# Batch 0's keys and queries by the software queue, cast on the way; memsets on VectorE; a written-out order table

## The chip, the cores and the metric

The kernel runs on one core of a Trainium2 chip. The metric is the device time of one execution in microseconds (us); three runs of the kernel before took 288.24 to 289.09 us, median 288.83 us. The core has five engines with an instruction stream each: PE (TensorE, matmuls), DVE (VectorE), ACT (ScalarE), POOL (GpSimd) and SP (SyncE). DMAs that SP issues go through a hardware queue (q1 in the profile), DMAs that POOL issues through a software queue (q0), whose descriptors POOL writes itself. Both queues share 16 DMA engines.

## The reference, cut to what matters

```python
def _attn_ref(q, k, v):                      # (8, 8, 576, 64): batch, heads, rows, head size
    scores = (1.0 / np.sqrt(D)) * np.matmul(q, k.transpose(0, 1, 3, 2))
    mask = block_i >= block_j                # blocks of 64 rows
    scores = np.where(mask, scores, -1e9)
    ...
    return np.matmul(softmax(scores), v)

def _moe_ref(x, w_tok1, w_tok2, w_ch1, w_ch2):   # x: (8, 576, 512), the heads side by side
    xt = x.transpose(0, 2, 1)
    h = np.maximum(xt @ w_tok1, 0.0) @ w_tok2    # over rows: 576 -> 256 -> 576
    u = x + h.transpose(0, 2, 1)
    h2 = np.maximum(u @ w_ch1, 0.0) @ w_ch2      # over channels: 512 -> 1536 -> 512
    return u + h2
```

All inputs and the output are float32 in DRAM. The kernel computes in bfloat16 with float32 sums.

## The kernel before

**The work.** Eight batches, each with attention over two groups of four heads (hg 0 and 1), a token mix and a channel stage of two products. For each head group, keys and queries lie as `qk_sb` tiles of 128 partitions (four heads, 32 partitions each) by 18 columns of 64 values, in bfloat16. DVE transposes them in blocks (`load_qk`, L540), by halves of nine columns. PE makes the scores in three sets (`score_set`, L664); ACT takes the exponential (`exp`, L682); PE multiplies with v (`head_out`, L712, and `ends_out`, L765); DVE divides by the row sum (L732, L738). Then come `token_up` (L906, L910), `first_uT` or `token_mix` (L939, L954, L1001), `channel_up` (L1125, later L1318) and the down products (L1547, L1452), whose results SP stores.

**Loads.** For batches 1 to 7, POOL issues one DMA per key or query tile (L517), and the DMA casts from float32 to bfloat16 on the way. For batch 0 (`first` in `load_qk`) SP issues nine float32 DMAs into staging tiles (L524; the stages are the `gT` tiles seen as float32, L350): halves of k and q, and the second half of q of hg 0 once more in two (edges 0, 9, 14, 18). ACT or DVE then casts each piece into `qk_sb` (L529, by way of the helper at L498 and L500), and DVE transposes it. All v (L566), token weights (L577) and channel weights (L600, L609) come by POOL's queue, cast on the way. At most eight POOL DMAs are in flight: the ninth waits for the landing of the first.

**Small things at the start.** POOL makes the identity (`make_identity`, L469), fills `bar` (two memsets), the pads of the first v tile (three) and the pads of the first token weight (two), all at L443, before it issues its first DMA. DVE fills `zeros` and the pads of the second v tile. `raise_clock` gives PE 16 matmuls over zeros (L469) and then up to 110 short ones of 256 columns (L476), "fillers", which stand in PE's stream where nothing else was ready.

**What sets the order.** `P.add` registers an op (a group of instructions on one engine) with its dependencies, a cost, a priority, and PSUM banks that it takes and gives. `Plan.placed` adds a table of shifts (`SHIFTS`) to the priorities and pins some ops to an engine (`ONLY`); `Plan.run` then goes through time by the costs, starts on each engine the ready op of best priority, and so fixes each engine's order, the engine of each op and its bank. The instructions are issued in that order, and each engine runs its own list in order; what the hardware waits for are semaphores. Fillers that found no room before 20 us are left out. The chip's real times do not change the order.

**Numbers of ops.** An op has the number of its `P.add` call. The text below uses the numbers of the table after the change, where the nine casts of batch 0 are gone and all later numbers are smaller by nine: 1, 3, 5, 7, 9 are the loads of hg 0 of batch 0 and 2, 4, 6, 8, 10 their transposes; 11, 13, 15, 17 the loads of hg 1 and 12, 14, 16, 18 their transposes; 19 to 23 and 24 to 28 the v loads; 29 to 39 the memsets, 40 the identity, 41 the 16 zero matmuls, 42 to 151 the fillers, 152 to 155 the token weights, 156 to 166 the channel weights, 171 and on the score sets, exponentials and head products of batch 0.

Of the kernel before, what the change touches and what calls it, by code (L numbers as in the profile page):

```python
# [11 lines left out]
FP32 = mybir.dt.float32  # L12
# [9 lines left out]
class Op:  # L22
# [3 lines left out]
        "engines", "cost", "deps", "emit", "prio", "take", "give", "xfer",  # L26
        "users", "need", "key", "waiting", "ready", "start", "end", "engine", "n", "mode", "at", "urgent", "until", "quick", "stick",
# [3 lines left out]
class Plan:  # L31


    LAG = {"PE": 0.28, "ACT": 0.2, "DVE": 0.18, "POOL": 0.22, "SP": 0.1}


    FIRST = {"POOL": 2.2, "ACT": 0.7, "SP": 0.7}
# [6 lines left out]
        for pool in pools  # L44
    }
# [8 lines left out]
    def add(  # L54
        self, engines, cost, emit, deps=(), prio=0.0, take=(), give=(), xfer=None, mode=0, at=0.0,
        urgent=0, until=1e9, quick=False, stick=False,
    ):

        o = Op()
        o.engines = (engines,) if isinstance(engines, str) else tuple(engines)  # L60
        o.cost = cost if isinstance(cost, dict) else {e: cost for e in o.engines}
        o.emit, o.prio, o.take, o.give, o.xfer = emit, prio, take, give, xfer
        o.mode, o.at, o.urgent, o.until, o.quick, o.stick = mode, at, urgent, until, quick, stick
        o.deps = list({id(d): d for d in deps if d is not None}.values())
        o.users, o.n = [], len(self.ops)
        self.ops.append(o)
        return o
# [4 lines left out]
    def fits(self, o, coming=()):  # L72
        for pools, n in o.need:
            have = sum(p in pools for p in coming)
            for p in pools:
                have += len(self.free[p])
            if have < n:
                return False
        return True

    def placed(self):

        letters = {"A": "ACT", "D": "DVE", "P": "POOL"}
        shifts, only = [int(x) for x in SHIFTS.split()], "".join(ONLY.split())
        assert len(self.ops) == len(shifts) == len(only)
        for o, shift, letter in zip(self.ops, shifts, only):
            o.prio += 0.05 * shift
            if letter in letters:
                o.engines = (letters[letter],)
        return self.run()  # L90

    def run(self):
        for o in self.ops:
            o.users = []
            o.need = [
                (pools, sum(set(other) <= set(pools) for other, _ in o.take)) for pools in {pools: 0 for pools, _ in o.take}
            ]
        for o in self.ops:
            o.waiting, o.ready = len(o.deps), o.at
            for d in o.deps:  # L100
                d.users.append(o)
        busy = {e: 0.0 for e in self.LAG}
        queued = [(o.at, o.n) for o in self.ops if not o.waiting]
        heapq.heapify(queued)

        avail = {e: [] for e in self.LAG}
        t, hard, soft, gives, order, mode = 0.0, 0.0, 0.0, [], [], 0
        left = len(self.ops)
        landed = [0.0] * 8

        fleeting = max([o.until for o in self.ops if o.until < 1e9], default=0.0)
        over = False
        while left:
            while queued and queued[0][0] <= t:
                o = self.ops[heapq.heappop(queued)[1]]
                o.key = (-o.urgent, o.prio, o.n, o)
                for e in o.engines:
                    bisect.insort(avail[e], o.key)
            while gives and gives[0][0] <= t:
                _, name, slot = heapq.heappop(gives)  # L120
                self.free[name].append(slot)
            began = False
            if not over:
                over = t > fleeting
                left -= sum(a[3].until < t for a in avail["PE"])
                avail["PE"] = [a for a in avail["PE"] if a[3].until >= t]
            for e in ("PE", "ACT", "DVE", "POOL", "SP"):
                if busy[e] > t or e == "POOL" and landed[-8] > t:
                    continue
                at = None  # L130
                tiled = e == "PE" and mode > 0
                for n, a in enumerate(avail[e]):
                    if a[3].stick > tiled or at is not None and not a[3].stick:
                        continue
                    if self.fits(a[3]):
                        at = n
                        if a[3].stick or not tiled:
                            break
                if at is None:
                    continue  # L140
                o = avail[e][at][3]
                soon = t + 0.6 * o.cost[e]
                if any(
                    r < soon and self.ops[n].urgent > o.urgent and e in self.ops[n].engines
                    for r, n in queued
                ):
                    continue
                if any(
                    -u[0] > o.urgent and self.fits(u[3], [name for r, name, _ in gives if r < soon])
                    for u in avail[e][:at]  # L150
                ):
                    continue
                for x in o.engines:
                    del avail[x][bisect.bisect_left(avail[x], o.key)]
                left -= 1
                began = True
                for pools, note in o.take:
                    note["pool"] = next(p for p in pools if self.free[p])
                    note["slot"] = self.free[note["pool"]].pop(0)
                o.engine, o.start = e, t  # L160
                o.end = busy[e] = t + o.cost[e] + 0.22 * sum(self.bare(note) for _, note in o.take)
                if o.mode is None:
                    o.mode = mode
                if e == "PE" and o.mode != mode:
                    o.end = busy[e] = o.end + 0.1
                    mode = o.mode
                order.append(o)
                lag = self.LAG[e]
                if o.xfer is not None:
                    first = o.end + self.FIRST[e]  # L170
                    if e == "POOL":
                        soft = max(soft, first) + o.xfer
                    else:
                        hard = max(hard, first) + o.xfer
                        soft += o.xfer * (soft > first)
                    o.end, lag = (soft if e == "POOL" else hard), 1.3
                    if e == "POOL":
                        landed.append(o.end + lag)
                for note in o.give:
                    to = self.TURN.get((note["pool"], note.get("covers")), note["pool"])  # L180
                    heapq.heappush(gives, (o.end + lag * (not o.quick), to, note["slot"]))
                for u in o.users:
                    same = u.engines == (e,) and o.xfer is None
                    u.ready = max(u.ready, o.end + ((e != "PE") * 0.05 if same else lag))
                    u.waiting -= 1
                    if not u.waiting:
                        heapq.heappush(queued, (u.ready, u.n))
            if not began:
                times = [b for b in busy.values() if b > t]
                times += [q[0] for q in queued[:1]] + [g[0] for g in gives[:1]] + landed[-8:]  # L190
                t = min(x for x in times if x > t)
        return order


SHIFTS = """
    0 0 0 1182 0 0 -172 0 0 186 0 0 -1226 0 0 1993 0 654 147 0 -1856 -1 0 -1627 2336 0 2272 -1123 -1113 -2707
    -2638 -1401 -798 -1583 -3531 -1120 -1939 -1736 0 0 0 0 0 -1021 -287 -489 0 0 0 0 0 0 0 0 0 0 0 0 0 0 0 0 0
    0 0 0 0 0 0 0 0 0 0 0 0 0 0 0 0 0 0 0 0 0 0 0 0 0 0 0 0 0 0 0 0 0 0 0 0 0 0 0 0 0 0 0 0 0 0 0 0 0 0 0 0 0
    0 0 0 0 0 0 0 0 0 0 0 0 0 0 0 0 0 0 0 0 0 0 0 0 0 0 0 0 0 0 0 0 0 0 0 0 0 0 0 0 0 0 0 0 0 -1629 -844 -738
    -987 -398 -755 -531 -696 -7 -19 -113 71 27 253 547 -2157 -341 -402 -3362 -1124 -1796 1135 -1317 2983 -860  # L200
    -4496 1412 484 -558 1057 -1890 -462 -3745 -4139 -1274 14 610 1601 3085 679 422 -1403 947 -248 2179 -1873
# [62 lines left out]
ONLY = """  # L264
# [17 lines left out]
def kernel(  # L282
# [11 lines left out]
    nc = tc.nc  # L294
# [1375 lines left out]
```

## Time and profile before

| what | value |
|---|---|
| time, three runs | 288.24, 288.83, 289.09 us |
| profiled execution: span from first to last instruction | 285.7 us (the page gives no other time of that execution; the median of the runs is 3.1 us above its span) |
| mean granted TensorE clock | 0.999 |
| PE busy | 280.5 us, 98% of the span |
| DVE, ACT, POOL busy | 234.5, 157.9, 69.6 us |
| software queue q0 | 44032 packets, 16.75 MB, 51.6% of 16 engines' span |
| hardware queue q1 | 20704 packets, 15.34 MB, 21.8% |

The page gives, for one execution, the busy time of each engine, the span in 40 slices, the DMA queues, and a chain of work followed back from the last instruction to whatever released each step. The trace can be asked for any stretch: a timeline lists instructions in order of time (start, duration, engine, line, operation, output<-input, and in brackets the idle time before it and what ended that), the chain of waits lists the steps of the chain (start, duration, what), and the view of a tile gives the time from the issue of its DMAs to their landing. A DMA instruction of POOL is busy while POOL writes descriptors; the data move later.

### The profile page before, as it was taken

The numbers are of one execution on the slowest core, as the hardware profiler recorded it, in microseconds if no ns is written. First come the engines' busy times: TensorE is split into PE (matmuls) and PEld (weight loads), VectorE is DVE, ScalarE is ACT, GpSimd is POOL, SyncE is SP. The second block draws the span as 40 slices with busy tenths as digits, with TensorE's granted clock in tenths as the row PEclk, the third lists the DMA queues.
The fourth block names the chain that finished last, engine by engine and source line by source line (L and its number), as shares of the span: only waits on it lengthen the run. The fifth ranks groups of instructions, "written<-read, shape, count | busy, mean of one in ns | idle before, by whom it ended". The sixth has DMA issues, their size and how long they took to land.

```text
span 285.7 us, 9042 instructions
## 1 busy us (share of the span) xinstructions
PE 280.5 (98%) x3923; PEld 188.2 (66%) x3923; DVE 234.5 (82%) x498; ACT 157.9 (55%) x212; POOL 69.6 (24%) x118
## 2 busy tenths in 40 slices
PE   8999999999999999999999999999999999999994
PEld 3676556565566856547876567744588985568883
DVE  3775788885699998479988588799996998999883
ACT  5986857568877458766475846335751037650000
POOL 8774545622251171701171001000000000000000
PEclk9999999999999999999999999999999999999999
DMA  8999999997499699942989006220080340000344
GB/s 228 215 165 208 213 182 186 206 183 151 66 100 105 82 197 204 187 54 22 136 137 199 6 2 76 76 92 2 19 129 2 117 179 0 0 2 0 149 127 169
DMA packets 64775, 32.65 MB, mean 114 GB/s; under 512 B 53088, under 2 KB 55264, under 8 KB 64736
## 3 DMA queue, kind: packets, MB, share of 16 engines
q0 software_dynamic: 44032, 16.75, 51.6%
q1 hardware_dynamic: 20704, 15.34, 21.8%
q8 instruction: 30, 0.49, 0.7%
q14 instruction: 9, 0.07, 0.1%
HBM read 35.85 MB, written 9.44 MB: 158 GB/s over the span
## 4 chain that ended last, share of the span: by engine, by line
PE 96%; DMA 1%; DVE 1%; SPq 0%; ACT 0%; issue 0%
PE mm L1452 17%; PE mm L1125 15%; PE sc L664 11%; PE late L1452 9%; PE mm L712 8%; PE late L1318 7%; PE mm L1318 6%; PE mm L906 5%; PE mm L1001 4%; PE mm L1547 4%; PE mm L765 2%; PE mm L1194 2%; DMA gT<-in_q_dram 1%; PE mm L910 1%; PE late L1194 1%; PE mm L476 1%
## 5 line engine op out<-in xcount | busy, mean ns | idle before, releaser
L682 ACT ACTIVATE e_sb<-sc 128x1024 bf16<-128x1024 f32 x95 | 92.4, 1023 | 40.9 <-PE sc L664 40.2
L540 DVE STREAM_TRANSPOSE qk_sb<-qk_sb 128x288 int32<-128x288 int32 (+1 forms) x65 | 41.2, 695 | 7.2 <-ACT qk_sb L498 4.0
L1125 PE MATMUL mm<-uT,wc_sb 128*128 128x512 bf16 x192 | 45.5, 381 | 0.0
L566 POOL DMA_DIRECT2D vals<-in_v_dram x45 | 37.2, 841 | 16.3 <-PE mm L712 7.3
L664 PE MATMUL sc<-qk_sb 32*64 32x64 bf16 (+7 forms) x1260 | 34.8, 293 | 0.2 <-DVE qk_sb L540 0.2
L1125 PEld LDWEIGHTS <-wc_sb 128*128 128x128 bf16 x192 | 20.2, 115 | 17.2 <-issue 1.3
L1452 PEld LDWEIGHTS <-sums 128*128 128x128 bf16 x288 | 27.7, 98 | 4.1 <-issue 0.9
L1452 PEld LDWEIGHTS <-gT 128*128 128x128 bf16 x288 | 27.5, 98 | 3.8
L664 PEld LDWEIGHTS <-qk_sb 32*64 32x64 bf16 x1280 | 19.6, 104 | 14.2 <-issue 9.0
L894 DVE TENSOR_SCALAR gT<-mm 128x512 bf16<-128x512 f32 x25 | 17.2, 687 | 13.9 <-PE mm L1125 13.2
L738 DVE TENSOR_TENSOR x_sb<-mm,rinv 128x256 bf16<-128x256 f32 x64 | 26.2, 421 | 1.5
L712 PE MATMUL mm<-vals,e_sb 128*128 128x65 bf16 x640 | 27.0, 193 | 0.1
L712 PEld LDWEIGHTS <-e_sb 128*128 128x128 bf16 x640 | 23.8, 97 | 4.8 <-issue 1.2
L892 ACT ACTIVATE gT<-mm 128x512 bf16<-128x512 f32 x35 | 20.5, 604 | 8.6 <-PE mm L1125 4.0
L498 ACT COPY mm<-late 128x512 f32<-128x512 f32 (+1 forms) x15 | 8.4, 563 | 26.3 <-PE late L1452 16.5
L906 PE MATMUL mm<-x_sb,w_sb 128*128 128x512 bf16 (+1 forms) x88 | 17.0, 321 | 0.0
L1016 DVE TENSOR_TENSOR u_sb<-mm,x_sb 128x512 bf16<-128x512 f32 x24 | 15.3, 680 | 1.4 <-PE mm L1001 1.2
L1452 PE MATMUL mm<-wd_sb,sums 128*128 128x256 bf16 x132 | 16.4, 273 | 0.0
L1318 PEld LDWEIGHTS <-ws_sb 128*128 128x128 bf16 x96 | 9.4, 98 | 9.9
L517 POOL DMA_DIRECT2D qk_sb<-in_k_dram x14 | 7.7, 553 | 32.8 <-DVE qk_sb L540 24.0
L1001 PE MATMUL mm<-aT,w_sb 128*128 128x512 bf16 x56 | 14.1, 380 | 0.0
L1452 PE MATMUL mm<-wc_sb,gT 128*128 128x256 bf16 x108 | 13.3, 273 | 0.0
(165 smaller groups left out, 481.8 us busy)
## 6 DMA issues: line engine op xcount, KB each, us to landing
out_dram<-o_sb SPq DMA_DIRECT2D x14, 512.0 KB, 3.4
qk_sb<-in_q_dram POOLq DMA_DIRECT2D x14, 288.0 KB, 6.3
qk_sb<-in_k_dram POOLq DMA_DIRECT2D x14, 288.0 KB, 6.9
vals<-in_v_dram POOLq DMA_DIRECT2D x28, 128.0 KB, 6.5
out_dram<-o_sb SPq DMA_DIRECT2D x7, 256.0 KB, 3.3
wc_sb<-in_moe_w_ch_dram POOLq DMA_DIRECT2D x8, 192.0 KB, 8.1
wc_sb<-in_moe_w_ch_dram POOLq DMA_DIRECT2D x3, 512.0 KB, 11.4
gT<-in_k_dram SPq DMA_DIRECT2D x4, 288.0 KB, 4.0
```

The source lines that it names most:

```text
L540: nc.vector.transpose(dst[:, 0:S, :] .rearrange("p s e -> p (s e)") .bitcast(I32) .rearrange("p (a k) -> p k a", k=NB)[:, k0:k1], raw2.bit ...
L566: nc.gpsimd.dma_start(out=t[128 - p : 128, J, hs, 0:64], in_=src)
L664: nc.tensor.matmul(out=home(n)[64 * half : 64 * half + 64, c : c + w], lhsT=bar[r, 0] if j is None else kT[i][r, 64 * j : 64 * j + 64, par ...
L682: nc.scalar.activation(dst, sc[SC.index(note["pool"])][:, :, 0:n], EXP, scale=scale)
L712: nc.tensor.matmul(out=u[:, I, 0:65], lhsT=e[:, h, c : c + 128], rhs=vt[:, J, head, 0:65], start=(J == 0), stop=(J == I),)
L738: nc.vector.tensor_tensor(out=xt[:, 0:4, 64 * head : 64 * head + 64], in0=u[:, :, 0:64], in1=ri[:, 0:4].to_broadcast([128, 4, 64]), op=MULT,)
L892: nc.scalar.activation(dst, src, RELU)
L906: nc.tensor.matmul(out=ps, lhsT=w1_sb[:, c, tt : tt + 255 : 2], rhs=xt[:, c, cols], start=(c == 0), stop=False)
L1001: nc.tensor.matmul(out=bank_of(bank), lhsT=w2_sb[:, t, 128 * si : 128 * si + 128], rhs=at[:, t, :], start=(t == 0), stop=(t == NDT - 1),)
L1125: nc.tensor.matmul(out=bank_of(bank), lhsT=wc1_sb[:, m, channels(cc)], rhs=uT[b % 2][:, :, m, :], start=(m == 0), stop=(m == NDM - 1),)
L1318: nc.tensor.matmul(out=bank_of(bank), lhsT=x(m), rhs=y[:, :, m, :], start=first and m == 0, stop=m == 1, skip_group_check=not first,)
L1452: nc.tensor.matmul(out=bank_of(bank)[:, 256 * i : 256 * i + 256], lhsT=x[:, kk, 128 * i : 128 * i + 128], rhs=y[:, kk], start=first and i ...
```

## The change

- In batch 0, each piece of k and q is loaded by POOL's queue straight into `qk_sb`, cast on the way. The staging tiles and the nine casts are gone; SP's nine loads become nine POOL loads.
- All seven memsets of POOL at L443 are now on DVE. The identity stays on POOL, with a later priority.
- `rinv` has nine tiles instead of four: one per head, and one for the ends. Reciprocals no longer wait for an earlier reader of their tile.
- The planner is gone. `Plan.placed` reads a table `ORDER` of words: number of the op, letter of its engine (T for PE, A, D, P, S), letters of the banks that it takes. The order, engines and banks of all ops of all batches come from that table.

```diff
-        fill("POOL", "bar", -1e6 + 1, (bar[:, 0, :], -BARRED), (bar[:, 1, :], 1.0))
+        fill("DVE", "bar", -1e5 + 1, (bar[:, 0, :], -BARRED), (bar[:, 1, :], 1.0))
...
-                ("POOL", "DVE")[i], ("v", i), (-1e5, -40)[i],
+                "DVE", ("v", i), (-1e5 + 2, -40)[i],
...
-        fill("POOL", "w1", -1e5 + 2, (w1_sb[64:128, 4, :], 0.0), (w1o_sb[0:64, :], 0.0))
+        fill("DVE", "w1", -1e5 + 3, (w1_sb[64:128, 4, :], 0.0), (w1o_sb[0:64, :], 0.0))
...
-        pads["ident"] = [P.add("POOL", 0.6, emit, (), -1e6)]
+        pads["ident"] = [P.add("POOL", 0.6, emit, (), -90)]
...
                 if first:
-                    def emit_load(o, k0=k0, k1=k1, hbm=hbm, st=st):
-                        nc.sync.dma_start(out=st[:, D * k0 : D * k1], in_=hbm[:, D * k0 : D * k1])
-
-                    ld = P.add("SP", 0.42, emit_load, (), -1e4 + n + 4 * hg, xfer=(0.1, 0.13)[hg] * (k1 - k0) - 0.47 * (hg + n + f == 0) + 0.6 * (hg == f == 0 and n == 1), at=0.7)
-
-                    def emit_cast(o, k0=k0, k1=k1, raw2=raw2, st=st):
-                        cast(o, raw2[:, D * k0 : D * k1], st[:, D * k0 : D * k1])
...
+                    def emit_load(o, k0=k0, k1=k1, hbm=hbm, raw2=raw2):
+                        nc.gpsimd.dma_start(out=raw2[:, D * k0 : D * k1], in_=hbm[:, D * k0 : D * k1])
+
+                    loads = [P.add("POOL", 0.55, emit_load, (), -1e4 + n + 4 * hg, xfer=0.0817 * (k1 - k0), at=0.72)]
...
-    rinv = ring(4, [128, 5, 1], FP32, "rinv")
-
-    stage = [t.rearrange("p c s -> p (c s)").bitcast(FP32) for t in gT]
+    rinv = ring(9, [128, 5, 1], FP32, "rinv")
...
-        ri = rinv[head % 3]
+        ri = rinv[head]
...
+ORDER = """
+    5P 37D 30D 29D 41Ta 1P 3P 7P 9P 11P 152P 6D 17P 2D 15P 33D 4D 13P 8D 21P 10D 42Td 22P 171Tsbc 194Tt 19P 172A
+    43Ta 44Ta 45Ta 46Ta 20P 47Ta 48Ta 49Ta 195A 173D 177Ts 34D 23P 32D 50Ta 12D 51Ta 52Ta 178A 175Tt 250P 18D 53Ta
+    54Ta 27P 39D 55Ta 176A 56Ta 38D 196Ts 16D 28P 57Ta 58Ta 14D 59Ta 197A 60Ta 61Ta 62Ta 174D 26P 63Ta 31D 209Tt
+    190A 213Ts 24P 191A 64Ta 179Td 25P 214A 180T 192D 183Ta 184T 193D 181D 202Tb 156P 203T 185D 210A 65Tc 182D 215Ts
...
+    392D 453Ta 408A 534P 393D 398P 451Tb 454D 528P 399Tst 394P 452A 369T 401A 523D 396P 521D 459Tc 400A 531P 390D
+    370T 460D 533P 455Ta 371A 430Tst 525P 456D 372S 469Tb 402P 431A 524D 457Tc 403P 461Td 470D 458D 465Ta 432A 463Tb
+    462D 466A 422Tc ...
```

## The prediction

> **What bounds the kernel now.** I read the page's busy times and its chain first, then the chain of waits of the first 40 us in order of time, then the timeline of the start, then the landings of the software queue.
>
> ```profile
> PE 280.5 (98%) x3923; PEld 188.2 (66%) x3923; DVE 234.5 (82%) x498; ACT 157.9 (55%) x212; POOL 69.6 (24%) x118
> ...
> PE 96%; DMA 1%; DVE 1%; SPq 0%; ACT 0%; issue 0%
> ```
>
> PE is busy nearly always, and almost the whole chain is PE's. A change of loads can gain only where the chain is not PE's own work. That is the start:
>
> ```profile
> 1.67 4.02 DMA gT<-in_q_dram
> 5.69 0.02 issue
> 5.71 0.68 ACT qk_sb L498
> 6.39 0.02 issue
> 6.42 1.40 DVE qk_sb L540 x3
> 7.81 0.04 issue
> 7.85 0.26 PE sc L664
> ...
> 8.98 0.87 PE mm L476 x7
> 9.86 0.58 PE sc L664 x12
> 10.43 0.33 PE mm L476 x2
> ...
> 13.67 0.54 PE mm L476 x4
> 14.21 0.30 PE mm L712 x10
> ```
>
> The first score waits for a load of q (landed 5.69), a cast, and three transposes, and begins at 7.85 us. After it come five groups of fillers (7, 2, 7, 2, 4; 2.94 us together), the last ending at 14.21. From there the chain is PE work to 281.9 us, and asked for PE's waits between 14 and 282 us the trace lists none. So the end is: the first score, plus a fixed sum of PE work, plus fillers, plus any stall that a new order brings. The stretch after the last matmul has the same last words in the table (last product, last fold, last store) and is left at nothing.
>
> ```profile
> 0.75 0.20 POOL masks.py:197 MEMSET ident<- 128x128 bf16 x1 [0.29 <-POOLq L1654]
> ...
> 2.85 5.83 POOL L566 DMA_DIRECT2D vals<-in_v_dram  x8
> ...
> 8.55 1.94 ACT L682 ACTIVATE e_sb<-sc 128x1024 bf16<-128x1024 f32 x2
> ```
>
> POOL can begin its own work at 0.75; its first DMA now waits behind identity and memsets until 2.85.
>
> **Step 1, the first score.** POOL now issues five loads of hg 0 first (words 5, 1, 3, 7, 9), from 0.75. One issue of a key or query load takes 0.55 us (L517). The nearest row for their flight is a tile load that met an otherwise empty software queue:
>
> ```profile
> L517 POOL DMA_DIRECT2D qk_sb<-in_k_dram x1: 545/545/545, 65.9 to 65.9; - x1
> ...
> DMA to landing us min/median/max: 3.7/3.7/3.7
> ```
>
> That is a whole tile of 288 KB; hg 0 needs two. Between 20 and 40 us, with the software queue alone, DMA moved 205 GB/s, so the second 288 KB take 1.44 us more: last landing 0.75 + 3.7 + 1.44 = 5.9 us. If the fifth issue sets it, it is 0.75 + 4 x 0.55 + 3.7 = 6.65 at most. Transposes follow piece by piece (0.72 us a half, 0.66 for the last two small ones), so the last ends at about 6.6 to 7.1. PE cannot begin sooner anyway: its 16 zero matmuls end at 6.71, and one filler stands behind them (0.12). I take 7.0: **-0.85 us**. The cast (0.68 us on the chain) is part of this, not extra. The bound on the bad side is the first v load (2.85, issued beside SP's loads at 315 GB/s in 2 to 6 us), which took 6.7 us to land: 0.75 + 6.7 + 1.44 gives 8.9, the first score at 9.3, +1.45 us. I lean to the first row, since the long one shared the DMA engines.
>
> **Step 2, the moved memsets and the casts.** POOL loses seven memsets (0.23 + 0.90 + 0.31 + 0.30 = 1.74 us) and the identity (0.5, now between DMAs, needed at L939, 22.2 us). DVE gains seven at 0.09 to 0.27 (its own L443 rows), 1.4 us at most, and loses three casts (0.45 + 0.70 + 0.43). Only word 33 stands between the transposes of hg 0, while the next piece is still in flight; without that cover it costs 0.1 to 0.2. ACT loses six casts (3.47 us), but its exponentials are paced by the first score: the first begins at 8.55, 0.70 behind it, and ACT is then full to 20 us. That lag stays. So step 2: 0.
>
> The trace has one row on DVE and POOL in each other's way: at 9.88 a weight load takes POOL 0.75 instead of 0.56, while a cast on DVE takes 0.70 instead of 0.45. The Trainium skill's page "SBUF — State Buffer", section "SBUF: two separate sides", says why such a change could lose: a VectorE instruction in a two-port mode locks POOL out, so that it can't write descriptors, and it advises the hardware queue. [...] The sum here doesn't use it, since no row shows a memset doing so.
>
> **Step 3, fillers and switches of form.** Before, 22 fillers run after the first score; the table has 23 (43 to 65). Groups of two and of seven cost 0.33 and 0.87, so one costs 0.108 and each group 0.114 on top, which is PE's change to another form of matmul and back. Going through PE's order I count changes between score, half-width and full forms: 125 before, 118 in the table. Seven fewer are 3.5 pairs x 0.114 = 0.40, or 0.80 if the 0.114 is one change. Less one filler: -0.29 to -0.69. I take **-0.3**.
>
> **Step 4, what is late next.** Hg 1 and v now queue behind hg 0 on one queue, with a 256 KB weight load (word 152) in between, which landed 2.2 us after the load ahead of it. Hg 1: 5.9 + 2.2 + 4 x 0.72 = 11.0 landed, transposed at 11.8. PE wants it (word 209) when the fourth exponential has freed its bank (1.0 each, L682, and 0.2 to PE), 7.0 + 0.70 + 4.2 = 11.9. Lateness up to 1.2 us is hidden, as two short exponentials (0.60 each) come first. The five v loads land 0.45 us apart (L566 at the start): 13.1; the first product with v comes about 14.0, behind seven score sets. Both fit by under 1 us, and both fall late with a late queue. The eight-in-flight limit holds word 15 back to the landing of word 5 (0.75 + 3.0), which is earlier than POOL gets there. SP's nine issues vanish, and with them 2.4 MB of float32 landings on q1; 1.2 MB join q0. The wider `rinv` takes waits away from an engine off the chain: 0. Some evacuations go from DVE to ACT (55% busy): 0.
>
> **The sum.** 285.7 - 0.85 - 0.3 = 284.55 us of span. The page's execution has no other time; the median is 3.1 us above its span, and I keep that: 288.83 - 1.15 = **287.7 us**.
>
> **Rivals.**
> Stall eats the gain: v of batch 2. In the table the last two v loads of batch 2 (394, 396) stand behind word 528, which waits for a transpose to free its tile, and the first product that reads them is 422. Between 396 and 422 PE has four pairs of L1001 (4 x 0.43), one part of L1547 (0.86), a score set (0.58), two groups of 128-column transposes (0.44) and one half-width product (0.85): 4.5 us. Software v loads land 3.4 us after issue at best, 6.1 at the median. At 5.5 (the stretch at 53 us) PE stalls 1.0: 288.7.
> **The slower side**, the same mechanism with the queue as it was late in the run:
>
> ```profile
> L566 POOL DMA_DIRECT2D vals<-in_v_dram x5: 690/888/896, 145.1 to 148.8; - x5
> ...
> DMA to landing us min/median/max: 6.1/7.1/7.4
> ```
>
> At 7.1 the stall is 2.6 at batch 2, and at batch 7 (word 960 to 979, 6.7 us of PE work by the same rows) about 0.5: 287.7 + 3.1 = 290.8. It turns the sign from a landing of 5.7 us on (4.5 + 1.15). For it: before had no wait to spare there and the table's lead is short. Against it: those 7.1 us are five loads in a row among SP's transfers, while 528 drains the queue first.
> The queue starts slowly, as the first v load did: +1.45 - 0.3 gives 290.0 at worst, and half of it, with the first piece late but the rest close behind, 289.2; I take 289.2. Against it: that row shared the engines. That the path doesn't change can't be: nine loads have another issuer in the diff.
>
> **Chances.** Forecast 0.55 (own range 287.0 to 288.2, one tenth of it within 0.3%); stall of about 1 us 0.13; slow start 0.14; slower side 0.18. A difference under 0.3%, 0.87 us, can hardly be told from none here: faster 0.50, same 0.05 + 0.13 + 0.14 = 0.32, slower 0.18. The range is 287.0 to 290.0: low end, 0.7 from switches and the earliest score; high end, the slow start at its worst; it leaves out most of the slower side.
>
> **What would show it.** Step 1: the chain's first score at 6.85 to 7.1 and no L498 ahead of it; wrong if POOL's loads land after 6.65. Step 2: first exponential 0.70 behind the score, ACT without a gap up to 20 us. Step 3: 24 fillers in all. Step 4: no idle time of PE ahead of word 209's scores, the first L712 and batch 2's ends. The prediction is wrong if PE lists waits on DVE or DMA after 14 us that sum to over 1 us.

## The result, and the profile after

The changed kernel took 293.18 us (median of 4 runs, 292.09 to 293.69), the kernel before on the same chip 288.6 (288.24 to 289.09): a ratio of 1.0162, 95% interval 1.0136 to 1.0188. It is slower by 4.6 us, where 287.7 was forecast with a range of 287.0 to 290.0. The profiled execution took 293.05 us, with a span of 291.0. So 2.05 us lie around the span. The kernel before has 1.9 to 2.0 there in the runs that list both times; the 3.1 us that the prediction kept was the distance of a median from the span of another, faster execution.

Busy times and the chain on the page of the changed kernel, to be held against the first fence of the prediction:

```profile
PE 280.4 (96%) x3916; PEld 187.9 (65%) x3916; DVE 228.1 (78%) x490; ACT 160.1 (55%) x215; POOL 73.4 (25%) x123
...
PE 79%; DMA 13%; POOL 5%; issue 1%; DVE 0%; POOLq 0%
```

PE is busy for the same 280 us, but 18% of the chain now are loads and POOL. What PE waits for is a list of its own, the wait view of PE (in total, times, longest):

```profile
PE mm L639 <- DMA vals<-in_v_dram: 2.5, 2, 1.9
PE sc L538 <- DVE qk_sb L414: 1.7, 2, 1.4
PE mm L355 <- DVE wd_sb L329: 1.2, 1, 1.2
PE mm L784 <- DMA w_sb<-in_moe_w_tok_dram: 1.0, 1, 1.0
PE mm L1421 <- DMA wc_sb<-in_moe_w_ch_dram: 0.4, 1, 0.4
```

The third line and 1.40 of the second lie ahead of the first score and cost nothing against before (first score at 7.78, before 7.85). The rest, 0.31 + 1.03 + 0.41 + 1.94 + 0.57 = 4.26 us, is new: before had no gap above 0.15 us behind the first score. The two largest are the first products that read v of batch 2, in the timeline of PE:

```profile
66.74 0.25 PE L639 MATMUL mm<-vals,e_sb 128*64 128x65 bf16 x4 [1.94 <-DMA vals<-in_v_dram]
67.56 0.25 PE L639 MATMUL mm<-vals,e_sb 128*64 128x65 bf16 x4 [0.57 <-DMA vals<-in_v_dram]
```

POOL's timeline shows why these loads were late:

```profile
50.39 0.31 POOL L569 MEMSET e_sb<- 64x256 bf16 x1 [7.58 <-DVE vals L564]
50.84 0.53 POOL L402 DMA_DIRECT2D qk_sb<-in_k_dram  x1
51.36 0.90 POOL L440 DMA_DIRECT2D vals<-in_v_dram  x1
52.25 0.56 POOL L402 DMA_DIRECT2D qk_sb<-in_q_dram  x1
56.13 3.35 POOL L440 DMA_DIRECT2D vals<-in_v_dram  x4 [3.32 <-PE sc L538]
59.44 0.59 POOL L402 DMA_DIRECT2D qk_sb<-in_q_dram  x1
59.99 2.68 POOL L440 DMA_DIRECT2D vals<-in_v_dram  x3
```

POOL stands still for 7.58 us at a small memset (word 294), then for 3.32 at word 532, a load of v for batch 3, which the trace shows waiting for PE. All five v loads of batch 2 stand behind the first, four of them behind the second. They are issued from 51.36 to 60.87 us; the last two (394, 396) land at 66.70 and 67.52, and PE wanted them at 64.80. In the kernel before, the same five were issued from 40.84 to 46.05, had landed by 53.78, and were first read at 62.07: 8.3 us to spare. Its rows, three of POOL and one of PE:

```profile
40.84 2.65 POOL L566 DMA_DIRECT2D vals<-in_v_dram  x3 [2.18 <-DMA wc_sb<-in_moe_w_ch_dram]
44.80 0.71 POOL L566 DMA_DIRECT2D vals<-in_v_dram  x1 [0.75 <-issue]
46.05 0.89 POOL L566 DMA_DIRECT2D vals<-in_v_dram  x1
...
62.07 0.77 PE L712 MATMUL mm<-vals,e_sb 128*128 128x65 bf16 x20
```

Then something that the waits do not list. The table of stretches (PE busy with its count, PEld, DVE, ACT, POOL, then granted clock, DMA share, GB/s):

```profile
64.80:67.60 2.80, 0.29 (x8) 0.20 (x9) 0.65 (x2) 0.89 (x2) 0.10 (x1) 1.00 1.93 231
67.60:69.00 1.40, 1.40 (x41) 0.93 (x41) 0.46 (x2) 0.29 (x1) 0.00 (x0) 1.00 1.89 211
69.00:72.40 3.40, 3.40 (x39) 2.30 (x37) 1.71 (x6) 1.65 (x2) 0.00 (x0) 0.50 0.58 88
```

PE stood idle for all but 0.29 us of 2.8, and 1.4 us after the idle time its granted clock went to half from 69.01 to 72.43, 3.41 us in which it did 1.7 us of work. The account of the two profiled spans: 291.0 - 285.7 = 5.3 = 4.26 (gaps) + 1.71 (clock) - 0.07 (first score) - 0.6 (the remainder; how much of it is what step 3 expected of fillers and forms isn't known).

The Trainium skill's page "TensorE: Matmul & The Clock Gate", section "HAM oscillation — how this bites in real kernels", puts the rule as no idle gaps of PE over about 3.4 us. The measurement is stricter: gaps of 1.94 and 0.57 with 0.25 us of matmuls between them were enough here. The length of the half-clock stretch, 3.41 us, is the window that the same page of the Trainium skill gives.

When the clock drops follows a grid. In the clock records of the traces, every stretch at half clock ahead of the end begins a whole number of 3.41 us after the first record of the full clock: 19 of them here (4.16 + 19 x 3.413 = 69.01), 18 in f2, 5 in f3, 4 in e4 and 1 in e3 (the runs are below). How much idle time in the 3.41 us before such a point takes the clock away is not settled by these traces. The first two of these stretches ended in half clock (in the changed kernel and in e4), the last two did not (in f5 and in f6):

```profile
65.60:69.01 3.41, 1.70 (x46) 1.15 (x46) 0.46 (x2) 0.39 (x2) 0.00 (x0) 1.00 1.83 242
17.43:20.85 3.42, 2.11 (x72) 1.65 (x65) 2.34 (x11) 2.77 (x3) 3.35 (x8) 1.00 1.39 134
42.77:46.18 3.41, 1.87 (x50) 0.94 (x49) 1.96 (x4) 2.38 (x3) 0.66 (x2) 1.00 2.19 171
5.67:9.08 3.41, 1.46 (x7) 0.59 (x6) 1.46 (x4) 1.47 (x3) 1.61 (x3) 1.00 1.31 259
```

PE was idle for 1.71, 1.31, 1.54 and 1.95 us in them, so idle time alone doesn't decide.

### The profile page after: what moved, and what is told of

Its sections match the earlier page's. It is cut to its first block, busy times and chain, and to the rows that moved or that the text cites. A ratio compares the mean times of both kernels' runs of the same rounds, so it can differ in the third digit from the quotient of the medians.

```text
span 291.0 us, 8988 instructions
## 1 busy us (share of the span) xinstructions
PE 280.4 (96%) x3916; PEld 187.9 (65%) x3916; DVE 228.1 (78%) x490; ACT 160.1 (55%) x215; POOL 73.4 (25%) x123
## 4 chain that ended last, share of the span: by engine, by line
PE 79%; DMA 13%; POOL 5%; issue 1%; DVE 0%; POOLq 0%
PE mm L1326 15%; PE mm L999 11%; PE late L1326 10%; DMA wc_sb<-in_moe_w_ch_dram 9%; PE sc L538 7%; PE late L1192 7%; PE mm L586 7%; PE mm L1192 6%; PE mm L780 3%; PE mm L875 3%; POOL vals L440 3%; DMA vals<-in_v_dram 2%; DMA w_sb<-in_moe_w_tok_dram 2%; PE mm L1421 2%; PE mm L1068 2%; PE mm L639 2%
## 5 line engine op out<-in xcount | busy, mean ns | idle before, releaser
L999 PE MATMUL mm<-uT,wc_sb 128*128 128x512 bf16 x192 | 47.4, 386 | 0.0
L586 PEld LDWEIGHTS <-e_sb 128*128 128x128 bf16 x640 | 24.6, 99 | 5.7 <-issue 2.0
L612 DVE TENSOR_TENSOR x_sb<-mm,rinv 128x256 bf16<-128x256 f32 x64 | 26.4, 421 | 1.6
L768 DVE TENSOR_SCALAR gT<-mm 128x512 bf16<-128x512 f32 x22 | 15.0, 687 | 9.2 <-PE mm L999 8.8
L606 DVE RECIPROCAL rinv<-mm 128x4 f32<-128x4 f32 x64 | 11.1, 176 | 10.3 <-PE mm L586 9.1
L890 DVE TENSOR_TENSOR u_sb<-mm,x_sb 128x512 bf16<-128x512 f32 x22 | 14.7, 685 | 2.9 <-PE mm L875 2.8
L780 PE MATMUL mm<-x_sb,w_sb 128*128 128x512 bf16 (+1 forms) x84 | 15.9, 318 | 0.0
L564 POOL COPY vals<-e_sb 128x256 bf16<-128x256 bf16 x10 | 4.8, 483 | 40.6 <-ACT e_sb L556 18.8
L384 ACT COPY mm<-late 128x512 f32<-128x512 f32 x12 | 6.9, 578 | 12.0 <-DVE sums L1308 4.9
```

What stands on the lines that cost most here:

```text
L586: nc.tensor.matmul(out=u[:, I, 0:65], lhsT=e[:, h, c : c + 128], rhs=vt[:, J, head, 0:65], start=(J == 0), stop=(J == I),)
L612: nc.vector.tensor_tensor(out=xt[:, 0:4, 64 * head : 64 * head + 64], in0=u[:, :, 0:64], in1=ri[:, 0:4].to_broadcast([128, 4, 64]), op=MULT,)
L780: nc.tensor.matmul(out=ps, lhsT=w1_sb[:, c, tt : tt + 255 : 2], rhs=xt[:, c, cols], start=(c == 0), stop=False)
L999: nc.tensor.matmul(out=bank_of(bank), lhsT=wc1_sb[:, m, channels(cc)], rhs=uT[b % 2][:, :, m, :], start=(m == 0), stop=(m == NDM - 1),)
```

## The experiments

All were compared with runs of the kernel before on their own chip, so ratios compare better between rows than times. "Idle" sums PE's gaps above 0.15 us behind the first score, and both it and the clock are of the profiled execution.

| kernel | time, us | ratio to before, 95% | first score | idle | clock |
|---|---|---|---|---|---|
| after | 293.18 | 1.0136 to 1.0188 | 7.78 | 4.26 | 0.994 |
| e1_v2_first | 289.4 | 1.0027 to 1.0073 | 8.52 | 1.37 | 0.999 |
| e2_fill_stall | 293.11 | 1.0144 to 1.0198 | 8.09 | 1.81 + fillers | 1.0 |
| e3_hw_loads | 297.16 | 1.0283 to 1.0348 | 10.78 | 2.44 | 0.988 |
| e4_no_stalls | 292.04 | 1.0113 to 1.0171 | 7.84 | 3.27 | 0.994 |
| f1_soft_old_order | 289.14 | 1.0011 to 1.0045 | 8.17 | 0.98 | 0.998 |
| f2_ident_first | 293.12 | 1.0141 to 1.0223 | 8.33 | 3.38 | 0.994 |
| f3_due_order | 291.7 | 1.0085 to 1.0166 | 7.88 | 2.51 | 0.994 |
| f5_due_order_dve | 291.99 | 1.0078 to 1.0155 | 8.56 | 2.27 | 1.0 |
| f6_due_hw | 290.73 | 1.0059 to 1.0117 | 9.65 | 1.95 | 1.0 |
| g1_mixed | 287.84 | 0.9953 to 0.9989 | 8.07 | 0 | 1.0 |
| g2_due_order_wc2 | 288.99 | 0.9998 to 1.0034 | 8.03 | 1.60 | 1.0 |
| h1_due_mixed | 287.71 | 0.9957 to 0.9986 | 7.44 | 1.08 | 1.0 |

### e1: v of batch 2 first

```diff
- 308D 532P 305D ... 409A 303D 395P 309D ... 534P 393D 398P 451Tb 454D 528P 399Tst 394P ... 523D 396P
+ 308D 395P 398P 394P 396P 532P 305D ... 534P ... 528P
```

> The kernel after the change with four words of POOL moved: the v loads 395, 398, 394, 396 of batch 2 now stand ahead of 532, 534 and 528, which wait for readers of other tiles. Everything else is as after. Theory (POOL's list): those v loads were late because they stood behind waiting words; issued some 4 us earlier they land ahead of PE's need, so PE's two gaps at 64.8 us (1.94 and 0.57) go, and with them the 3.4 us at half clock that follow (1.7 us lost). Time 293.2 - 4.2 = 289.0, clock 0.999. Rival 1 (the queue's data: batch 0's loads put the software queue behind for good): the loads land when the queue comes to them, the gap stays at 1.5 us or more, time 292 to 293.5. Rival 2 (the gap matters, the clock doesn't): 290.7.

Measured: 289.4. One edit of four words gives back 3.8 of the 4.6 us by the medians, and 3.2 by the two ratios to before (1.0162 and 1.0050; the executions of e1 spread from 288.7 to 291.5, and one at a clock of 0.98 took 293.3). A row of POOL and a row of PE with the words moved:

```profile
53.89 5.10 POOL L439 DMA_DIRECT2D vals<-in_v_dram  x6 [0.89 <-issue]
...
64.82 0.29 PE L638 MATMUL mm<-vals,e_sb 128*64 128x65 bf16 x8
```

The four moved loads are the first of these six. They start at 53.89 and have landed by 62.62, and PE finds all of v at 64.82 and runs on. No stretch at half clock near 69 us is left. Matched instruction by instruction, the changed kernel's PE is ahead of e1's up to 64.8 (0.74 at the first score, which differs between executions), is 2.68 behind after both gaps, 4.2 behind at the end of the half clock, and 3.8 from 73 us to the last matmul. Nothing after 73 us matters for the difference. The memset 294 stayed where it was, and POOL issued its next load at 51.03, about as in the changed kernel (50.84): the places behind 532, 534 and 528 are what made the loads too late.

### e2: the same stall, filled

```diff
- 466A 422Tc
+ 466A 66Tc 67Tc ... 83Tc 422Tc
```

> The kernel after the change with 18 more fillers (66 to 83, 0.107 us each, 1.9 us together) put on PE just ahead of 422, the first product that waits for batch 2's v. The wait for v stays, but PE works through the first gap. Theory (idleness drops the clock): no stretch at half clock after 67 us, time 293.2 - 1.7 = 291.5, the gap ahead of L639 under 0.3 us. Rival (the clock drops for another reason, or the drop costs nothing): the half clock stays, time 293.2 or up to 0.3 more.

Measured: 293.11. The 18 fillers ran from 64.92 to 67.06, the gap behind them was 0.30, and the profiled execution has no half clock. Its PE runs 2.2 us behind e1's from 70 us on, where the changed kernel's is 3.8 behind: 1.6 better, the size of the half clock. That fits idleness as what takes the clock away, as theory had it: all six executions have a clock of 0.996 or more, the four of the changed kernel 0.992 to 0.994. But the time is that of the changed kernel, not the 291.5 of the theory, and three of six executions at a clock of 1.0 took 293.2 to 293.9. Where those spent it isn't known, since only the one of 292.17 left a trace. As a measure of what the half clock costs the run is inconclusive.

### e3: the new table with hardware loads

```diff
- 5P 37D 30D 29D 41Ta 1P 3P 7P 9P 11P 152P 6D 17P ...
+ 5S 1S 3S 7S 9S 11S 17S 15S 13S 37D 30D 29D 41Ta 152P (casts: 5, 1, 3, 7, 9, 11 on A, 17, 15, 13 on D) 6D ...
```

The staging tiles and the nine casts come back (six on ACT, three on DVE); all other words stay.

> The kernel after the change with batch 0's keys and queries loaded as before (nine loads by SP into staging tiles, nine casts: six on ACT, three on DVE), everything else in the table's order. Theory (POOL's list of the table is the loss, not the way of the loads): the gaps ahead of batch 2's v products and the half clock stay, time 292 to 294, first score at 7.7 to 8.0. Rival (the loads on the software queue are the loss): the gaps at 20, 44 and 65 us go, time 288 to 289.

Measured: 297.16, as neither theory had it. The trace is of the fastest execution (294.64, clock 0.988); the other four took 297.1 to 297.7 at 0.975 or 0.976. SP's timeline in e3, and then in the kernel before, from the issue that stalls in the one and not in the other:

```profile
3.63 3.20 SPq L420 DMA_DIRECT2D gT<-in_q_dram  x2
```

```profile
4.04 0.91 SPq L524 DMA_DIRECT2D gT<-in_q_dram  x2
```

With nothing ahead of it on POOL, the 256 KB token weight is issued at 1.25 and v from 2.13. SP's pieces of hg 0 then land from 3.65 to 9.85 (before, from 3.72 to 6.92), two issues of SP take 3.20 instead of 0.91, the first score starts at 10.78, and the clock is at half from 9.24 to 16.07. In the kernel before, POOL's memsets and identity keep POOL's first load back to 2.85. Whether that delay alone protects SP's loads was not tried by itself.

### e4: every gap's load earlier

```diff
  (e1, and)  155P 153P ahead of 250P; 17P 15P 13P ahead of 152P; 166P behind 165P
```

> As the kernel with batch 2's v loads moved, and also: the small token weights 155 and 153 ahead of batch 1's first query load (250), batch 0's loads of hg 1 (17, 15, 13) ahead of the 256 KB token weight (152), and the last channel weight (166) right behind 165. Theory: all five gaps of PE after the first score go (0.31, 1.03, 0.41, 1.94, 0.57 = 4.26 us) and the half clock (1.7 us): 293.2 - 6.0 = 287.2, under the kernel before by 1.4. Rival (the moved words make others late): a new gap on PE appears behind a load that was pushed back, time 288.5 to 290.

Measured: 292.04; the mechanism is the rival's, the time is above both ranges. Gaps at the token weights and at hg 1 go, and gaps of 0.80 and 1.26 at v of batch 0 come, the second followed by half clock from 20.85 to 24.26. A gap of 1.05 ahead of 72.25 has no releaser in the trace. The software queue has no slack in these 20 us: what went ahead made v late.

### f1: the change without its table

```diff
- (the changed kernel's ORDER)
+ 1P 3P 5P 7P 9P 11P 13P 15P 17P 37D 30D 29D 33D 34D 36D 35D 0A 41Ta 20P 21P 2D 25P ...
```

All other words are those that the planner of before put out, with the casts left out and the identity ahead of word 157.

> The change without its table: batch 0's keys and queries by the software queue without staging and casts, the memsets on VectorE, but every engine's words in the order that the kernel before had (POOL: the nine pieces ahead of the v loads; the identity just ahead of the channel weights). Theory (the order table lost the time, the load path is worth about nothing): 288.5, 287.8 to 289.3, TensorE idle only ahead of the first score, no half clock near 69 us, span about 286. Rival (the load path itself costs: the pieces issued one after another by POOL and the v loads behind them come late): 290 or more, with gaps where v of batch 0 is first used, between 12 and 22 us.

Measured: 289.14, 0.7 above before. So the load path with the moved memsets and the nine `rinv` tiles costs about 0.7 in the old order, and on this load path the table makes the rest of the 4.6 us. The two shares hold in this order only: with loads by SP the table was worse still (e3). There is no gap at v of batch 2: this order issues its loads from 42.20 to 48.04 us, they land by 55.52, and PE reads them from 63.54 on. The table leaves the reading where it was and puts the loads 9 to 13 us later, behind the memset and batch 3's loads.

### f2: the identity first

```diff
+ 40P 5P 37D ...     (40P no longer ahead of 157P)
```

> The changed kernel with one word moved: the identity is made on POOL ahead of the first load, as the kernel before has it. Theory (the first load of POOL starts at 1.25 because the software queue is not ready earlier, not because of what POOL runs): identity at 0.75 to 1.25, first load at 1.25 to 1.4, time as the changed kernel, 293. Rival (POOL's own work sets it): first load at 1.75 to 1.85, first score 0.5 later, 293.5 to 294.

Measured: 293.12. The identity ran at 0.75 to 1.31, as in before, and the first load started at 1.44 instead of 1.25, closer to the theory (1.25 to 1.4) than to the rival (1.75). POOL's queue takes its first load 0.5 us later than its first memset, and 0.56 us of POOL work ahead of it costs 0.19. The first score came 0.55 later, as the rival had it, but it also came 0.74 later in e1 and 0.31 later in e2, whose starts are unchanged, so it tells nothing here. Why the first load isn't taken earlier is open: in every run VectorE's first memset ran from 0.87 to 1.14, and no run moved that memset.

### f3 and f5: loads by due time, and one DVE word

```diff
  (e1, and POOL's first words, each in the next place of the list)
+ 5P 1P 3P 7P 9P 11P 17P 15P 13P 21P 22P 19P 20P 23P 152P 27P 28P 26P 24P 25P 155P 153P 250P 156P 154P
  (and 166P ahead of 261P; f5 besides:)
- 208D 232Ts 251D 40P ... 159P 226D
+ 208D 232Ts 40P ... 159P 251D 226D
```

> The first experiment (v of batch 2 ahead of v of batch 3) and POOL's first 25 loads sorted by when they are wanted: the three pieces of the second head group and v of the first ahead of the large token weight, v of the second, then the small token weights, then batch 1's first keys; the third piece of the second channel weight two loads earlier. Theory (each left-over gap of the first experiment, 0.41, 0.42 and 0.28, is a load in the wrong place): 288.4, 287.6 to 289, no gap above 0.2 between 9 and 64 us. Rival (the queue has no room, so each load put earlier makes another late, as in the fourth experiment): gaps of 0.5 or more at the token weights or at batch 1's first scores, 289.5 to 291.

Measured: 291.7, above both ranges. Every gap that e1 left is gone, and there is one new one, where neither theory had put it. Waits of PE, then of DVE between 14 and 26 us:

```profile
PE mm L638 <- DVE x_sb L611: 2.5, 1, 2.5
```

```profile
DVE qk_sb L413 <- DMA qk_sb<-in_q_dram: 2.7, 1, 2.7
```

DVE stood at word 251, a transpose for batch 1, whose load I had moved back; the divisions of batch 0's heads stood behind it, and PE behind those. Then 23.0 to 26.4 us ran at half clock, 1.6 us after the gap had ended.

> The sorted loads of f3 with one word of VectorE moved: the transpose of batch 1's first keys, 251, for whose load VectorE stood still for 2.71 while four divisions of finished heads stood behind it, goes 25 VectorE words later. Theory (that one wait on VectorE made TensorE's gap of 2.51, and the gap made the half clock from 21.4 on, worth another 1.7): 291.7 - 2.5 - 1.7 = 287.5, 287.0 to 288.1, no gap above 0.3 after the first score and full clock throughout; faster than the kernel before. Rival (the first 30 us are short of loads, whoever waits): a gap of 1 or more at the token weights or at v, and 289 to 290.5.

The word moved by 7 VectorE words, not 25.

Measured: 291.99, but the six executions fall apart by their clock: 290.09 and 290.12 at 1.0, 291.35 at 0.997, 292.64 to 293.00 at 0.991 or 0.992. The gap of 2.51 is gone. But 1.54 came at 44.5, where word 166, which I had put ahead of batch 1's key load 261, made that load land at 44.10, DVE stand for 4.93 at its transpose, and PE wait for the evacuation (DVE's copy of a product out of PSUM) behind it. The forecast of 287.5 was wrong. The two executions at full clock lie in the rival's range, but the gap of over 1 us came at 44.5, not in the first 30 us, and was made by another of my moves. The executions also give a size for the clock: 0.008 of 291 us are 2.3 us, and those near 0.992 took 2.5 to 2.9 more. Only the one of 290.09 left a trace, so what else the slower ones lost isn't known.

### f6: the due order with hardware loads

```diff
- (f5) 5P 1P 3P 7P 9P 11P 17P 15P 13P
+ 40P 5S 1S 3S 7S 9S 11S 17S 15S 13S, and the nine casts as in e3
```

> The same table with batch 0's keys and queries by SP's queue into staging tiles and nine casts (six on ScalarE, three on VectorE), as before, and the identity ahead of POOL's first load. Theory (by hardware the load path is worth what the change without its table lost, 0.7, and v of batch 0, now ahead of the large token weight, doesn't disturb SP's loads for long): 286.8 to 287.6, first score at 7.8 to 8.3. Rival (POOL's loads, begun at 1.4 instead of 2.85, take the DMA engines from SP's, as in the third experiment): first score at 9 to 11, 288.5 to 292.

Measured: 290.73, first score 9.65: the rival. With POOL's first load at 1.44 instead of 2.85, SP's five pieces of hg 0 land by 8.72 instead of 6.92. PE stood idle for 2.52 ahead of the first score, and the clock stayed at full.

### g2: one load back

```diff
- (f5) 165P 166P 261P 382P
+ 165P 261P 382P 166P
```

> f5 with one word moved back: the third piece of the second channel weight (166) again behind the loads 261 and 382. In f5 it went ahead of them, batch 1's key load 261 landed at 44.10, VectorE stood still for 4.93 at that key's transpose, and TensorE waited 1.54 for the evacuation behind it. Theory (the DMA queue has no room here, so whatever goes ahead makes the next late): that gap goes, one of 0.2 to 0.45 at the weight itself comes back, 288.8 to 289.3 in executions at a clock of 1.0 and 1.5 to 2.9 more in those near 0.992. Rival (the gap was the execution's own, not the word's): a gap of 1 or more near 44 us stays, 290 to 292.

Measured: 288.99, as the theory had it: the gap near 44 us is 0.15, at the weight itself; the largest left is 0.90 ahead of 22.01, where PE waits for VectorE. With four moves on POOL and one on DVE the table stands where the old order does (f1, 289.14).

### g1 and h1: the first two pieces by hardware

```diff
- (f1) 1P 3P 5P 7P 9P ...                  (h1: the same in g2)
+ 1S 3S 5P 7P 9P ..., 2001A 2003A          casts of 1 and 3 on ACT; transposes 2D 6D 4D 8D 10D
```

> The change without its table (f1), but the two key pieces of the first head group come by SP's queue into staging and are cast on ScalarE, beside the other seven, which stay on the software queue. A try for a version below both kernels. Theory (the start is bound by landings: one queue brings five pieces in 4.5 to 7.6 there, two queues bring hardware pieces at 3.7 and 4.4 and software pieces at 4.5, 5.2 and 5.9, so the first score starts at 7.2 to 7.5 instead of 8.17): 288.2 to 288.7, as the kernel before within 0.2%. Rival (the queues share the DMA engines, as in the third experiment): first score at 8 to 8.5 and 289 to 289.6, as f1.

Measured: 287.84, 0.9 below before and 1.3 below f1, below what I had forecast. The first score did not move as the theory said:

```profile
6.99 1.15 PE L371 MATMUL mm<-wd_sb 128*128 128x256 bf16 x9
8.07 0.42 PE L562 MATMUL sc<-qk_sb 32*64 32x512 bf16 x4
```

The transposes ended at 7.41, but this order puts nine fillers ahead of the first score, which so starts at 8.07, in the rival's place. The gain lies further on: v of batch 0 comes earlier than in f1 (the first load landed at 10.14, there 11.98; the fifth at 11.90, there 13.85; the eighth at 13.98, there 14.61), and f1's lag of 1.2 us against before, built up between 26 and 52 us in gaps of 0.19 to 0.27, does not arise. PE has no gap behind the first score. That the earlier v is what takes that lag away was not tried by itself.

> The mended table of g2 with the start of g1: the two key pieces of the first head group by SP's queue and a cast on ScalarE, the other seven by the software queue. Theory (the mixed start is worth what it was from f1 to g1, 1.3, whatever the table, because it frees 1.0 of POOL's issue time and brings v about 2 earlier): 287.5 to 288.2. Rival (in g1 it paid because that table has its v loads spread over 14 us; here the gaps at 6.65 and 21.11 are set by VectorE's transposes, not by landings): 288.6 to 289.2, as g2.

Measured: 287.71. Here one filler stands ahead of the first score, which starts at 7.44. Both are faster than the kernel before by 0.3% (intervals 0.11 to 0.47% and 0.14 to 0.43%), and so than the changed one; between the two no difference can be told.

## Why the prediction was wrong

The step that failed is the one that set PE's waits behind the first score at nothing, and with it the claim that both checks of step 4 fit. PE waited 4.26 us behind late loads there, 2.51 of it for v of batch 2, and lost 1.71 more at half clock, a term that the sum didn't have. Step 1 failed too: it gained 0.07 instead of 0.85. The steps in turn:

- **What bounds the kernel.** Right as a description of before. The step "a fixed sum of PE work plus any stall that a new order brings" was right, too, but I searched two places for stalls. The whole order was new.
- **Step 1, first score at 7.0: failed.** It started at 7.78. The first issue was taken at 1.25, not 0.75, since POOL's first memset is no row for its first DMA. The flight of the first piece was 3.31, better than the 3.7 taken. But the five landings spread over 2.70 us (4.56 to 7.26), where 1.44 were taken for the second half; the queue moved 178 GB/s between 4 and 7 us instead of 205. Of the two landings worked out, the later one (fifth issue plus 3.7, 6.65) was the right form: the fifth issue came at 3.51 instead of 2.95, which alone makes it 7.21. DVE's last transposes ended at 7.73. Worth 0.07, not 0.85.
- **Step 2, nothing.** Held within 0.1: the first exponential began 0.76 behind the score (0.70 taken). ACT, expected without a gap up to 20, ran on to 14.5 us and had gaps of 0.27 and 0.40 up to 21.
- **Step 3, -0.3.** One filler before the first score and 23 after, as counted. The account leaves 0.6 for it and for all else; it was not tested alone.
- **Step 4: failed, and it decided.** Hg 1 landed at 12.67 instead of 11.0, and PE waited 0.31. V of batch 0 landed by 14.87 instead of 13.1 (whose own terms give 13.2), and PE did not wait. The token weights 155 and 153, which the table put behind 250 and 156, I had not looked at: they landed at 21.31 and cost 1.03. The second channel weight cost 0.41.
- **The slower rival had the place and the size, and half of the mechanism.** It asked for a landing 7.1 us after issue and priced batch 2 at 2.6; the two loads took 6.7 and cost 2.51. I named word 528 as what stands ahead of them; POOL did not wait at 528 at all, and 294 and 532 held it for 10.9 us. What spoke against the rival, "528 drains the queue first", did not happen: the queue was nearly idle while POOL stood still (38 GB/s from 50 to 51.6 us), but when 394 was issued five loads had gone out in the 3.9 us before it. Its 0.5 at batch 7 did not come either. What lifts its 290.8 to 293.2 is the half clock (1.7), the gaps of 1.03, 0.41 and 0.31, and that step 1's gain, on which it was built, never came; against these stand the 0.5 of batch 7 and 1.1 of the offset. A chance of 0.18 for it was too low: the cover of 4.5 us was set against quick landings instead of the rows late in the run. And "before had no wait to spare there" was not so: it had 8.3 us to spare, which the table gave up. The timeline of before and the table, side by side, would have shown that drop. That the rival's 290.8 falls short of the result by only 2.4 is in part luck, since some of what it lacked is offset by what it had too much of.
- **The offset.** The 3.1 us were 2.0 between a span and its own time, and 1.1 between executions.

## What to carry to other kernels

An engine with an in-order list that issues loads needs a due-time check of every load against every wait ahead of it in that list, its own and those of other engines' words. The longest waits here were at instructions that nobody needed yet. Compare how long each load lies ready before its use in the old order and in the new one, and go through all consumers after each move, since on a full queue an advance can be paid by another load (e4, f5). A short stall of TensorE can be worth more than its length: look at the granted clock of the next few microseconds before you price it.

## What the runs showed of the hardware

- TensorE's clock dropped to half for 3.41 us (in e3 for 6.83) at points a whole number of 3.41 us after the first record of the full clock, with 1.71 us (changed kernel), 1.84 (f2), 1.78 (f3), 1.31 (e4) and 2.04 (e3) of idle time in the 3.41 us before. With 1.95 (f6), 1.65 and 1.54 (f5) it did not drop, so idle time alone doesn't tell. Between executions of f5, a clock of 0.991 to 0.992 instead of 1.0 went with 2.5 to 2.9 us.
- POOL's first instruction of the program's work starts at 0.75 us if it is a memset, at 1.25 if it is a DMA; an identity of 0.56 ahead moves the DMA to 1.44 only (f2).
- Two queues at the start help each other or harm each other by what they carry: two key pieces on SP beside seven on POOL gained 1.3 us (g1 against f1), and all nine on SP beside POOL's weights and v put the first score back to 9.65 and 10.78 (f6, e3), where the kernel before, with POOL's first load at 2.85, had 7.85.
